# A small constant added to the softmax row sums by ACT instead of DVE, for the first twelve heads

## The chip, the core and the metric

The kernel runs on one core of a Trainium2 chip. The engines are named as in the profile: PE is TensorE (matrix products and transposes), DVE is VectorE, ACT is ScalarE, POOL is GpSimd, and SP is the queue from which nearly all transfers are issued. Each engine works through its own queue of instructions and waits on semaphores for what other engines or transfers deliver. The metric is the time of one execution on the device, in microseconds, as the median of several runs.

## The reference

Attention with a sliding window and a few always visible first keys ("sinks"), followed by a two-layer network:

```
scores = scale * q @ k.T                     # 4 batches, 8 heads, 768 positions, head size 64
keep = (key < n_sink) | (0 <= pos - key < window)      # n_sink 4, window 128
a = exp(where(keep, scores, -1e9) - max)
a = a / (sum(a) + 1e-09)
x = (a @ v) laid out as 3072 x 512
h = x @ w_in                                 # 512 x 2048
g = max(h, 0) + log1p(exp(-abs(h)))
out = g @ w_out                              # 2048 x 512, float32
```

The sum of `1e-09` and the row sum is the place of the change. The weights come in as 64-bit floats; all else is 32-bit.

## The kernel before

The 768 positions of each batch are cut into three chunks of 256 queries, twelve chunks in all, and each chunk is worked on as two blocks of 128 rows (j = 0, 1). A query block needs only its own 128 keys, the 128 before them, and the sinks, which fit into 136 columns since the two key blocks are folded into one by a mask (`copy_predicated`, line 270).

For one head h of a chunk the steps are named by letters:

- S, `scores`: PE multiplies queries and keys of both blocks into PSUM.
- T, `softmax` (lines 259 to 277): DVE folds and masks the scores and takes the row maximum into `stats` (lines 270, 276); ACT takes the exponential and sums each row into a column of `sm`, a 128 x 2 tile with one column for each block (line 277: an ACTIVATE and a read of the accumulator for each block).
- N, `normalise` (lines 279 to 291): DVE adds 1e-9 to `sm` (line 283) and takes the reciprocal into `rc` (line 284); then POOL, ACT or DVE multiplies the weights of both blocks by it (lines 289, 291), as a string of letters (`Ctx.NM`) says for each head; for heads 0 to 11 that is P P V A P A P P P A V P.
- W, `weights_t`: PE transposes the weights, ACT or DVE copies them out of PSUM into `th` (`Ctx.TH`), POOL selects the triangles into `pt`.
- k and K: the same for the sink columns. V, `values`: PE multiplies with the values. O, `out`: the result is split into a high part `xh` (ACT) and a low part `xl` (DVE or POOL).

The network part of a chunk has the steps U (first product), F (three ACT functions on a 128 x 512 tile), P and R (DVE's sum, the high part `gh` and the residue `gl`), D and E (second product). All products with 32-bit values run as sums of products of high and low parts.

The weights are turned into such parts only once, during the first chunks, in 32 halves (wi for the first layer, wo for the second): w issues the transfer on SP, a copies out the upper 16 bits (`upper`), c puts together a 32-bit word on DVE (line 434), d rounds it to the high part and l subtracts for the low part, on engines named by the strings `WT`, `WH` and `WL`.

The order is written out by hand. `Ctx.START` is a list of such letters with head numbers, for everything up to the point where a regular pattern (`Ctx.STEADY`) takes over, and every engine's queue keeps that order. Its beginning, which holds the twelve heads of the change (N0 to N11; heads 8 to 11 are the first four of the second chunk):

```
j4 w w w J0 S0 T0 G4 w S1 S2 w N0 L8 T1 T2 S3 w N1 L10 S4 W1 T3 a N2 W0 w T4 a N3 S5 k0 c c K0 a S6
w d c T5 d V0 V1 l N4 l W2 T6 w d O0 a G6 c S7 W3 O1 l N5 N6 T7 z18 V2 a a c N7 d W4 k4 S8 a T8 O2 w V3
c S9 c O3 w w K4 d a l l W5 V4 T9 S10 W6 L12 N9 V5 O4 d T10 w l N8 O5 W7 G8 d S11 w c T11 l a V6 V7
G10 a L14 N11 N10 O6 k8 w w c W8 O7 U0 d c l a d S12 ...
```

G and L are loads of values and of queries and keys, issued on SP in the same order as the weight transfers; z are products that fill PE's idle time. `sm` has two buffers, `rc` two.

Of the kernel before, what the change touches and what calls it, by code (L numbers as in the profile page):

```python
# [11 lines left out]
F32 = mybir.dt.float32  # L12
# [5 lines left out]
AF = mybir.ActivationFunctionType  # L18
ALU = mybir.AluOpType

B, H, S, D = 4, 8, 768, 64
DM, DFF = 512, 2048
P = 128
# [35 lines left out]
def _zero(nc, out, finite):  # L59
    nc.gpsimd.tensor_scalar(out, finite, 0.0, 0.0, ALU.mult, ALU.add)  # L60


def _turn(engines, k):

    return engines[min(k, len(engines) - 1)]
# [57 lines left out]
class _Attention:  # L123
# [155 lines left out]
    def normalise(self, h):  # L279
        c, nc = self.c, self.c.nc  # L280
        g, hh = h // G, h % G
        rc, sm = self.rc[g][:, :, hh], self.sm.pop(h)
        nc.vector.tensor_scalar(sm[:], sm[:], 1e-9, None, ALU.add)
        nc.vector.reciprocal(rc, sm[:])  # L284
        for j in range(CH):
            a = self.a[g][:, hh, j, :P]
            eng = _turn(c.NM, self.chunk * H + h)
            if eng == "A":
                nc.scalar.mul(a, a, rc[:, j : j + 1])
            else:  # L290
                (nc.vector if eng == "V" else nc.gpsimd).tensor_scalar(a, a, rc[:, j : j + 1], 0.0, ALU.mult, ALU.add)  # L291
# [544 lines left out]
def _general(c):  # L836

    tc, nc = c.tc, c.nc
    with ExitStack() as st:
        pool = lambda n, bufs: st.enter_context(tc.tile_pool(name=n, bufs=bufs))  # L840
        psum = lambda n, bufs: st.enter_context(tc.tile_pool(name=n, bufs=bufs, space=bass.MemoryType.PSUM))
        c.stg, c.gp, c.xp, c.mp = pool("gstg", 2), pool("gp", 1), pool("gxp", 1), pool("gmp", 1)
        c.ps_acc, c.ps_h, c.gs, c.gt, c.gx = psum("gacc", 1), psum("gh", 1), psum("gs", 1), psum("gt", 1), psum("gx", 1)
        _general_weights(c)
        keep = _general_masks(c)
        with tc.For_i(0, B, 1) as b:
            for n in range(NCH):
                xh, xl = c.x[n] = [c.xp.tile([P, 4, CT], F32R, tag=f"x{e}", name=f"gx{e}{n}") for e in "hl"]
                for h in range(H):
                    if h % 2 == 0:  # L850
                        xt = c.gx.tile([P, CT], F32, name=f"g_x{n}_{h}", tag="g_x")
                    _general_head(c, b, n, h, keep, xt)
                    if h % 2 == 1:
                        _copy(nc, "A", xh[:, h // 2], xt[:])
                        _sub(nc, "V", xl[:, h // 2], xt[:], xh[:, h // 2])
                m = _Moe(c, n)
                m.row = b * S + n * CT
                for s in range(FP):
                    m.up(s)
                    m.softplus(s)  # L860
                    m.gate(s)
                    m.residue(s)
                    for j in range(2):
                        m.down(s, j)


def _kernel(tc, a, out):
    nc = tc.nc
    c = Ctx()
    c.nc, c.tc, c.a, c.out = nc, tc, a, out  # L870
    c.E = dict(qkh="A", ql="V", kl="V", vh="A", vl="P", xh="A", xl="P", gl="V", out="AV")
    c.x, c.vs, c.vst, c.vsr, c.vsh = {}, {}, {}, {}, {}
    c.w64 = a["w"].dtype == mybir.dt.int64
    nc.scalar.preload_act_table_set("natural_log_exp_and_others")
    with ExitStack() as keep:
        c.const = keep.enter_context(tc.tile_pool(name="const", bufs=1))
        c.wp = keep.enter_context(tc.tile_pool(name="wp", bufs=1))
        c.w, c.raw, c.top, c.word = {}, {}, {}, {}
        c.ident = c.const.tile([P, P], F32, name="ident")
        c.stats = c.const.tile([P, B * H * NB], F32, name="stats")  # L880
        c.room = c.const.tile([P, 2, 4 * FP], F32, name="room")
        nc.gpsimd.memset(c.room[:], 1.0)
        c.sk = c.const.tile([P, CT], F32R, name="sk")
        ones = c.room[:].rearrange("p a b -> p (a b)").unsqueeze(1).broadcast_to([P, CT // 64, 64])
        _zero(nc, c.sk[:].rearrange("p (a b) -> p a b", b=64), ones)
        with ExitStack() as st:
            pool = lambda n, bufs: st.enter_context(tc.tile_pool(name=n, bufs=bufs))
            psum = lambda n, bufs: st.enter_context(tc.tile_pool(name=n, bufs=bufs, space=bass.MemoryType.PSUM))
            c.xp, c.mp, c.stg = pool("xp", 2), pool("mp", 2), pool("stg", 4)
            c.lp, c.ap, c.sp = pool("lp", 2), pool("ap", 2), pool("sp", 2)  # L890
            c.ps_acc, c.ps_h = psum("ps_acc", 1), psum("ps_h", 2)
            c.ps_s, c.ps_t, c.ps_x = psum("ps_s", 2), psum("ps_t", 1), psum("ps_x", 1)
            c.last = True
            with tc.manual_schedule(engines=ORDERED):
                _fast(c)
            c.last = False
        ok = nc.values_load(c.flag[:1, :1], min_val=0, max_val=1)
        with tc.If(ok < 1):
            _general(c)


Ctx.nchunks = B * NCH
Ctx.GB, Ctx.EXACT = 3, 2
Ctx.NM = "PPVAPAPPPAVPPAPVP"
Ctx.TH = "AAVVAAAAVAAAAAVVVA"
Ctx.GH = "AAVAVPPVV"
# [20 lines left out]
def build(nc, a, out):  # L927
    with tile.TileContext(nc, schedule_with_timeline_sim=True) as tc:
        _kernel(tc, a, out)
# [55 lines left out]
```

## Time and profile before

| what | value |
|---|---|
| median of 3 runs | 714.65 us (714.27 to 715.22) |
| the profiled execution's own time | 715.5 us |
| its span, first to last instruction | 713.7 us |
| PE busy | 691.6 us, 97% of the span |
| DVE busy | 574.2 us, 80% |
| ACT busy | 451.3 us, 63% |
| POOL busy | 373.7 us, 52% |
| granted TensorE clock | 0.997 of full speed |

Durations below are from the one profiled execution. A row of the timeline names the start in us from the span's start, the duration, the engine, the line of the kernel, the operation, what is written from what is read, and in brackets the idle time of the engine just before it with what ended that. Shares of busy time over the whole span mix the first part, in which weights are converted and the heads of the first chunks start, with the long regular part; the stretches are therefore read apart.

### The profile page before, as it was taken

Reading aid. Unit: us, or ns where it says so; the run is one execution under the profiler, and the core shown is the slowest. Engines: PE = TensorE matmul, PEld = TensorE weight load, DVE = VectorE, ACT = ScalarE, POOL = GpSimd, SP = SyncE. Lnnn points to the kernel's source line nnn. Section 1 sums busy time; section 2 is a strip of 40 time slices with the busy share of each in tenths; the row PEclk is TensorE's granted clock in tenths of the full one; section 3 lists DMA queues with packets and bytes.
Section 4 is the critical chain, followed back from the end, with each engine's and each line's share of the span. In section 5 each row is a group of like instructions: output and inputs, shape, how many; then the busy total and the mean of one; then the engine's idle time right before and its main releaser. Section 6 shows DMA issues by size and latency. Waiting matters only on the chain.

```text
span 713.7 us, 13800 instructions
## 1 busy us (share of the span) xinstructions
PE 691.6 (97%) x4519; PEld 624.8 (88%) x4519; DVE 574.2 (80%) x1663; ACT 451.3 (63%) x1105; POOL 373.7 (52%) x676
## 2 busy tenths in 40 slices
PE   6789899999999999999999999999999999999996
PEld 5678799989989999998999999998998989999995
DVE  5899988888888987888887887988888888865541
ACT  4679857667666666666666666766665765753431
POOL 5867586655555564654645554664554555452000
PEclk9999999999999999999999999999999999999998
DMA  8987613122221311411321321322222222100001
GB/s 308 326 329 237 209 51 98 52 73 77 63 76 56 97 50 50 124 52 46 102 68 49 109 63 56 93 65 65 76 76 66 83 62 67 61 12 1 30 1 35
DMA packets 39483, 64.52 MB, mean 90 GB/s; under 512 B 4650, under 2 KB 20074, under 8 KB 39402
## 3 DMA queue, kind: packets, MB, share of 16 engines
q1 hardware_dynamic: 38826, 63.02, 28.1%
q8 instruction: 38, 0.62, 0.4%
q10 hardware_dynamic: 576, 0.53, 0.2%
q14 instruction: 43, 0.35, 0.2%
HBM read 57.24 MB, written 6.29 MB: 89 GB/s over the span
## 4 chain that ended last, share of the span: by engine, by line
PE 89%; DMA 5%; ACT 2%; DVE 1%; POOL 1%; SPq 1%; issue 0%; POOLq 0%; DVEq 0%; ACTq 0%
PE h L490 37%; PE acc L541 12%; PE acc L542 12%; PE acc L543 12%; PE x L364 6%; PE s L255 3%; PE s L256 3%; PE t L324 2%; PE x L357 1%; DMA wi50r<-w 1%; DMA wo21r<-w 1%; DMA wi01r<-w 1%; DMA wo70r<-w 1%; DMA vz<-v 1%; PE ts L308 1%; ACT upper L48 0%
## 5 line engine op out<-in xcount | busy, mean ns | idle before, releaser
L490 PE MATMUL h<-xh,wi 128*128 128x256 f32 x1536 | 253.6, 288 | 0.0
L490 PEld LDWEIGHTS h<-xh,wi 128*128 128x128 f32 x1536 | 211.2, 191 | 0.9
L291 POOL TENSOR_SCALAR a<-a,rc 128x128 f32<-128x128 f32 x178 | 69.1, 401 | 188.8 <-DVE rc L284 156.1
L490 PE MATMUL h<-xl,wi 128*128 128x256 f32 x768 | 154.7, 283 | 0.0
L541 PE MATMUL acc<-wo,gh 128*128 128x512 f32 x384 | 151.9, 396 | 0.0
L543 PE MATMUL acc<-wo,gl 128*128 128x512 f32 x384 | 150.8, 393 | 0.7 <-DVE gl L56 0.7
L542 PE MATMUL acc<-wo,gh 128*128 128x512 f32 x384 | 150.8, 393 | 0.0
L490 PEld LDWEIGHTS h<-xl,wi 128*128 128x128 f32 x768 | 119.6, 192 | 0.0
L497 ACT ACTIVATE mt<-h 128x512 f32<-128x512 f32 x96 | 57.1, 595 | 97.5 <-PE h L490 97.4
L505 DVE SCALAR_TENSOR_TENSOR mt<-h,mt 128x512 f32<-128x512 f32 x96 | 66.1, 689 | 62.9 <-ACT mt L499 55.4
L277 ACT ACTIVATE a<-a,stats 128x136 f32<-128x136 f32 x192 | 76.2, 398 | 42.3 <-DVE stats L276 42.2
L543 PEld LDWEIGHTS acc<-wo,gl 128*128 128x128 f32 x384 | 72.2, 188 | 17.6 <-DVE gl L56 1.1
L541 PEld LDWEIGHTS acc<-wo,gh 128*128 128x128 f32 x384 | 72.2, 188 | 12.5
L542 PEld LDWEIGHTS acc<-wo,gh 128*128 128x128 f32 x384 | 72.4, 188 | 8.8
L56 DVE TENSOR_TENSOR gl<-mt,gh 128x512 fp32r<-128x512 f32 x96 | 79.4, 827 | 0.3
L335 POOL TENSOR_SCALAR_AFFINE_SELECT pt<-tl 128x256 fp32r<-128x256 f32 x80 | 60.0, 749 | 23.4 <-DVE tl L56 22.8
L498 ACT ACTIVATE mt<-mt 128x512 f32<-128x512 f32 x96 | 60.7, 633 | 3.1
L499 ACT ACTIVATE mt<-mt 128x512 f32<-128x512 f32 x96 | 60.7, 632 | 3.1
L335 POOL TENSOR_SCALAR_AFFINE_SELECT pt<-th 128x256 fp32r<-128x256 f32 (+1 forms) x96 | 43.7, 456 | 35.6 <-ACT th L48 32.7
L48 ACT CAST qkh<-qk 128x656 fp32r<-128x656 f32 x80 | 59.5, 744 | 2.0 <-DMA qk<-qk 2.0
L56 DVE TENSOR_TENSOR kl<-qk,qkh 128x400 fp32r<-128x400 f32 x80 | 51.6, 645 | 2.5
L56 DVE TENSOR_TENSOR tl<-t,th 128x256 f32<-128x256 f32 x80 | 33.2, 414 | 23.3 <-ACT th L48 23.3
(187 smaller groups left out, 1235.0 us busy)
## 6 DMA issues: line engine op xcount, KB each, us to landing
qk<-qk SPq DMA_DIRECT2D x160, 164.0 KB, 3.0
out<-o SPq DMA_DIRECT2D x23, 256.0 KB, 2.3
vr<-v SPq DMA_DIRECT2D x28, 192.0 KB, 2.6
q<-q SPq DMA_DIRECT2D x7, 256.0 KB, 5.5
k<-k SPq DMA_DIRECT2D x8, 200.0 KB, 4.8
vz<-v SPq DMA_DIRECT2D x4, 384.0 KB, 5.1
vr<-v SPq DMA_DIRECT2D x12, 128.0 KB, 2.3
vz<-v SPq DMA_DIRECT2D x4, 256.0 KB, 5.6
```

The lines of the kernel that those rows point to most:

```text
L48: nc.scalar.copy(out, in_)
L56: (nc.vector if eng == "V" else nc.gpsimd).tensor_tensor(out, a, b, ALU.subtract)
L277: nc.scalar.activation(a, a, AF.Exp, bias=nm, scale=-1.0, accum_out=sm[:, j : j + 1])
L291: (nc.vector if eng == "V" else nc.gpsimd).tensor_scalar(a, a, rc[:, j : j + 1], 0.0, ALU.mult, ALU.add)
L335: nc.gpsimd.affine_select(pt[:, e, :, 1], src[:], [[0, CH], [1, P]], ALU.is_ge, 0.0, base=0, channel_multiplier=-1)
L490: nc.tensor.matmul(h[:, j], wt, x, start=k == 0, stop=k >= len(prods) - 2, skip_group_check=True)
L498: nc.scalar.activation(t[:], t[:], AF.Exp, scale=-1.0)
L499: nc.scalar.activation(t[:], t[:], AF.Ln, bias=1.0)
L505: nc.vector.scalar_tensor_tensor(t[:], h[:], 0.0, t[:], ALU.max, ALU.add)
L541: nc.tensor.matmul(acc[:], gh[:, j, q], wh, start=f == 0, stop=False, skip_group_check=True)
L542: nc.tensor.matmul(acc[:], gh[:, j, q], wl, start=False, stop=False, skip_group_check=True)
L543: nc.tensor.matmul(acc[:], gl[:, j, q], wh, start=False, stop=f == 2 * FP - 1, skip_group_check=True)
```

## The change

For the first twelve heads, counted over chunks, ACT adds the constant: an Identity whose bias is a column filled once by POOL. All other heads keep DVE's add. The reciprocal stays on DVE.

```
         rc, sm = self.rc[g][:, :, hh], self.sm.pop(h)
-        nc.vector.tensor_scalar(sm[:], sm[:], 1e-9, None, ALU.add)
+        if self.chunk * H + h < c.SA:
+            nc.scalar.activation(sm[:], sm[:], AF.Identity, bias=c.eps[:, 0:1])
+        else:
+            nc.vector.tensor_scalar(sm[:], sm[:], 1e-9, None, ALU.add)
         nc.vector.reciprocal(rc, sm[:])
...
         nc.gpsimd.memset(c.room[:], 1.0)
+        c.eps = c.const.tile([P, 1], F32, name="eps")
+        nc.gpsimd.memset(c.eps[:], 1e-9)
...
-Ctx.GB, Ctx.EXACT = 3, 2
+Ctx.GB, Ctx.EXACT, Ctx.SA = 3, 2, 12
```

Neither `Ctx.START` nor any other order is edited; the Identity stands in ACT's queue where N_h stands in the list.

## The prediction

> **What bounds the kernel now.** I read the busy time of each engine in stretches first, then the chain of waits, then who waited for whom, and last the instructions of DVE and ACT in order of time up to 40 us.
>
> ```profile
> 39.00:87.00 48.00, 42.45 (x274) 37.29 (x274) 47.10 (x105) 41.88 (x89) 29.62 (x33) 1.00 0.74 254
> 87.00:640.00 553.00, 553.00 (x3681) 504.06 (x3681) 466.45 (x1359) 362.44 (x898) 311.32 (x573) 1.00 0.24 70
> ```
>
> The columns are the stretch, its length, then the busy time of PE, PE's weight loads, DVE, ACT and POOL, the granted clock, the DMA share and GB/s. From 87 to 640 us PE is busy for the whole 553.00 us: there nothing that DVE or ACT does is felt. From 39 to 87 us PE is not full (42.45 of 48.00), and DVE is (47.10). So the end is set by when PE's unbroken stretch begins, and that by DVE. The waits confirm both ends; first those of PE from 87 us to the end, then those of DVE from 38 to 95 us:
>
> ```profile
> PE x L364 <- POOL pt L338: 0.3, 1, 0.3
> ```
> ```profile
> DVE xl L56 <- ACT xh L48: 0.3, 1, 0.3
> ```
>
> PE's last wait of the whole run is 0.3 us long, at the start of the window. DVE waits 0.3 us in all between 38 and 95 us. Whatever DVE is late by at 39 us it therefore carries to 87 us, and PE with it to the end, unless something else was later still.
>
> **Where the changed instructions lie.** The add of line 283, for the window from 0 to 38.1 us:
>
> ```profile
> L283 DVE TENSOR_SCALAR sm<-sm x12: 149/170/608, 9.6 to 38.0; 128x2 f32<-128x2 f32 x12
> ```
>
> All twelve heads, N0 to N11 in the written order, are normalised before 38.1 us, ahead of the stretch in which DVE never rests. Nothing in the steady part is touched. What remains is what DVE and ACT do between 9 and 39 us; here are the rows that the sum uses, DVE's first. The columns are start, duration, engine, line, operation, operands and count.
>
> ```profile
> 9.63 0.17 DVE L283 TENSOR_SCALAR sm<-sm 128x2 f32<-128x2 f32 x1 [0.74 <-ACT a L277]
> 9.83 0.17 DVE L284 RECIPROCAL rc<-sm 128x2 f32<-128x2 f32 x1
> ...
> 11.56 0.17 DVE L284 RECIPROCAL rc<-sm 128x2 f32<-128x2 f32 x1
> ...
> 12.47 0.17 DVE L284 RECIPROCAL rc<-sm 128x2 f32<-128x2 f32 x1
> ...
> 13.49 0.08 DVE L276 DVE_READ_ACCUMULATOR2_ANT stats<- 128x1 f32 x1
> ...
> 14.68 0.52 DVE L50 CAST upper<-wi01r 128x512 f16<-128x512 bf16 x1 [0.89 <-DMA wi01r<-w]
> ...
> 15.51 0.17 DVE L284 RECIPROCAL rc<-sm 128x2 f32<-128x2 f32 x1
> ...
> 19.50 0.17 DVE L284 RECIPROCAL rc<-sm 128x2 f32<-128x2 f32 x1
> ...
> 23.81 0.28 DVE L283 TENSOR_SCALAR sm<-sm 128x2 f32<-128x2 f32 x1
> 24.12 0.17 DVE L284 RECIPROCAL rc<-sm 128x2 f32<-128x2 f32 x1
> ...
> 24.39 0.17 DVE L284 RECIPROCAL rc<-sm 128x2 f32<-128x2 f32 x1
> ...
> 32.52 0.17 DVE L284 RECIPROCAL rc<-sm 128x2 f32<-128x2 f32 x1
> ...
> 34.84 0.42 DVE L56 TENSOR_TENSOR xl<-x,xh 128x256 fp32r<-128x256 f32 x1 [0.71 <-ACT xh L48]
> ...
> 38.16 0.17 DVE L284 RECIPROCAL rc<-sm 128x2 f32<-128x2 f32 x1
> ```
> ```profile
> 11.92 0.18 ACT L277 ACTIVATION_READ_ACCUMULATOR a<-a,stats 128x1 f32 x1
> 13.03 0.37 ACT L48 COPY th<-t 128x256 f32<-128x256 f32 x1 [0.93 <-PE t L324]
> 13.30 0.41 ACT L277 ACTIVATE a<-a,stats 128x136 f32<-128x136 f32 x1
> ...
> 14.00 0.19 ACT L277 ACTIVATION_READ_ACCUMULATOR a<-a,stats 128x1 f32 x1
> ...
> 19.56 0.60 ACT L48 CAST wi<-wt 128x512 fp32r<-128x512 f32 x1
> ...
> 24.39 0.69 ACT L289 ACTIVATE a<-a,rc 128x128 f32<-128x128 f32 x2 [2.72 <-DVE sm L283]
> ...
> 32.78 0.37 ACT L48 COPY th<-t 128x256 f32<-128x256 f32 x1 [0.58 <-PE t L324]
> ...
> 34.46 0.35 ACT L48 CAST xh<-x 128x256 fp32r<-128x256 f32 x1
> ...
> 37.44 0.77 ACT L48 CAST upper<-wo11r 128x512 f16<-128x512 bf16 x1
> ...
> 47.47 0.62 ACT L48 CAST gh<-mt 128x512 fp32r<-128x512 f32 x1
> 48.00 0.79 ACT L48 CAST upper<-wo21r 128x512 f16<-128x512 bf16 x1
> ```
>
> The reader is to see that ACT's queue runs in the written order. Head 3's exponential begins at 13.30, behind the copy of W1 at 13.03, for which ACT sat idle 0.93 us waiting for PE, although DVE had moved on long before. An instruction put into ACT's queue at N_h is thus held by all that is written ahead of N_h: by the exponentials of a later head, and by copies that wait for PE.
>
> **The price of one Identity.** No Identity of this size is in the trace. From below, the smallest ACT row is the accumulator read (0.18 us at 11.92); from above, the multiply with a column operand, two of which fill 0.69 us at 24.39, on 128 columns instead of 2:
>
> ```profile
> L48 ACT CAST xh<-xf 128x256 fp32r<-128x256 f32 x40 | 16.3, 406 | 44.0 <-DVE xf L383 44.0
> L48 ACT CAST wi<-wt 128x512 fp32r<-128x512 f32 x11 | 6.7, 610 | 1.0 <-DVE wt L434 1.0
> L289 ACT ACTIVATE a<-a,rc 128x128 f32<-128x128 f32 x8 | 2.8, 394 | 3.2 <-DVE sm L283 2.7 <-DVE rc L284 0.4
> L874 ACT ACT_TABLE_LOAD x1 | 1.3, 1283 | 0.8 <-PEq L978 0.8
> ```
>
> One more column costs (610 - 406)/256 = 0.80 ns, so 126 fewer than the multiply's 394 ns leave 0.29 us. I take 0.29, with 0.19 and 0.39 as ends. After it the reciprocal starts 0.03 us later, as it did after the add (9.63 + 0.17 = 9.80, then 9.83): 0.32 us from the Identity's start. The next independent ACT instruction starts 0.10 us before its predecessor's end, as at 13.03 + 0.37 and 13.30.
>
> [...]
>
> **The change, head by head.** I push each step by the lateness so far, keep all other spacings, and write the lateness of the reciprocal against its old start.
>
> N0: the Identity takes the add's moment, 9.63; reciprocal at 9.95, late 0.12.
> N1 is written behind T1 and T2, so it stands behind the exponential of head 2, whose last read moves to 12.04. Identity 12.14, reciprocal 12.46 (was 11.56): late 0.90. POOL's normalisation of head 1, PE's transpose and ACT's copy of it (13.03) move with it, and so does head 3's exponential behind that copy, whose last read comes at 14.90.
> N2 is written behind T3, hence behind this exponential: Identity 15.00, reciprocal 15.32 (was 12.47): late 2.85. Before, the add of head 2 waited for nothing. Queued behind the waiting reciprocal on DVE are T4, the weight conversions and all later heads.
> N3 stands behind head 4's exponential. T4's first statistic is out at 13.57 + 2.85 = 16.42, the pair takes 0.70 to its last read (13.30 to 14.00): 17.15; Identity 17.25, reciprocal 17.57 (was 15.51): late 2.06. Part of the lateness is absorbed here, because the old DVE stood 0.89 us before 14.68 for a DMA.
> N4 stands behind the weight cast that ran at 19.56: that is 21.62 now, the Identity starts 22.12, reciprocal 22.44 (was 19.50): late 2.94.
> N5 finds its Identity done. DVE comes at 23.81 + 2.94 = 26.75 and goes on at once. N6 stands behind ACT's two multiplies of head 5, which wait for N5's reciprocal: they start 0.27 after it as before (24.12 to 24.39), at 27.02, and let go 0.59 later; Identity 27.61, reciprocal 27.93 (was 24.39): late 3.54.
> N7 finds its Identity done; the add's 0.20 (9.63 to 9.83) comes back: 3.34.
> N9 is written behind W6, whose copy ran at 32.78: 36.12, next instruction 36.39, reciprocal 36.71 (was 32.52): late 4.19.
> N8 is written behind T10 and takes the place of the cast at 34.46, now 38.65; the cast moves to 38.84, and the subtraction that waited for it (34.84) is late 4.38. The reciprocal, at 38.97, is not what DVE waits for last.
> N11 and N10 stand behind the conversion of 37.44: 41.82 plus 0.67, Identities at 42.49 and 42.68, reciprocal of N10 at 43.00 (was 38.16): late 4.84.
>
> DVE is thus 4.8 us late when its unresting stretch begins. The Identity's duration enters this some ten times (N0 to N4, N6, N9, N8 and both of the last pair), so its ends give 3.8 and 5.8. The constant column is one more memset of POOL at the start. I cost it at nothing: nobody reads it before the first Identity at 9.63, where DVE sits waiting anyway (0.74 us in its row); without that cover it would cost its own length, which no row shows for one column and which I bound by the 0.17 us of DVE's add. SP issues no new DMA, but its loads of later heads wait for PE's scores of earlier ones and move with DVE by 2 to 4 us.
>
> The profiled execution took 715.5 us around a span of 713.7; with 4.8 more it is a span of 718.5 and a time of 720.3. The three runs have their median 0.85 below the profiled one, at 714.65, so the forecast there is **719.4 us**.
>
> **Rivals.** A: DVE is relieved and the kernel is faster. Each add held DVE 0.20 us, twelve of them 2.4, and the slowest (608 ns) some 0.4 more: 712.0. [...] For it speaks that DVE is full and ACT is not. It holds where ACT has passed N_h before DVE comes, and in the rows that is so for N5 and N7 alone. It would decide if ACT's queue did not hold the Identities back. Chance 0.09.
>
> B: The weight DMAs decide from 39 us on, so only their delay counts. The chain of waits says this:
>
> ```profile
> 31.37 7.99 DMA wo21r<-w
> 39.36 0.02 issue
> 39.38 8.64 DMA wi50r<-w
> 48.02 0.77 ACT upper L48
> ```
>
> The delay would be that of the loads issued behind T5, 2.06 us: 716.7. Against it, the instruction at 48.00 converts wo21r, landed at 39.36, and ACT was busy right up to it (47.47 + 0.62 - 0.10 = 47.99); nothing waited there. Chance 0.10.
>
> C: No change, because something I hold to be in step with DVE had slack and swallows the 4.8 us. DVE's waits above show 0.3 us of it. 714.6, chance 0.07.
>
> D: Identity is not in the loaded table set, and each one brings two table loads of 1.28 us: about ten on the path, 26 us, 740. The multiplies of line 289 ran with one load in the whole trace. Chance 0.02.
>
> **How the numbers follow.** The forecast has the remaining 0.72. The range takes in its ends (718.4 and 720.4) with some 0.8 more above for shifted collisions on DVE, whose adds vary from 149 to 608 ns, and rival B below with 0.5 for the same reason: 716.2 to 721.2. Outside lie A, C and D, 0.18. A measurement of this kernel can tell 0.2%, 1.4 us, from no change. Slower than that are the forecast, B and D: 0.84; same 0.07; faster 0.09.
>
> **What would show it.** Right: DVE's reciprocals wait for ACT some 10 us in all before 45 us, where the adds waited for two exponentials before; the longest single wait, over 2 us, stands at N2 behind head 3's exponential; the reciprocal of N10 starts near 43.0; from there all rows are the old ones shifted by one amount, and PE's last wait lies near 91.5 us. Wrong: the Identities start out of the written order, or the shift at N10 is 4.8 us and that at PE's last wait much smaller, or the reciprocals come earlier than before.

## The result, and the profile after

The changed kernel takes 721.63 us (median of six runs, 720.17 to 723.55) against 714.46 us before (six runs beside them): +7.2 us, a ratio of 1.0104 [1.0093, 1.0115]. It is slower. The forecast was 719.4 with a range up to 721.2; the time lies 0.4 above that range. The profiled execution took 722.55 us around a span of 720.7 and a mean granted clock of 0.993 (before: 715.5, 713.7, 0.997).

First the busy time in stretches, in the same columns as before:

```profile
9.00:39.00 30.00, 20.67 (x101) 16.36 (x100) 19.11 (x78) 17.31 (x64) 16.96 (x34) 0.89 0.84 305
39.00:87.00 48.00, 40.68 (x254) 34.99 (x253) 45.51 (x114) 41.43 (x97) 30.56 (x37) 1.00 0.77 265
87.00:100.00 13.00, 12.73 (x87) 11.62 (x87) 12.73 (x30) 11.34 (x24) 9.34 (x11) 1.00 0.32 90
100.00:640.00 540.00, 540.00 (x3595) 491.81 (x3594) 456.18 (x1334) 354.21 (x878) 305.05 (x561) 1.00 0.24 71
```

The steady part is as it was: PE is busy for the whole of 100 to 640 us. The loss lies in the first row. Its clock column reads 0.89, which the prediction had not reckoned with. The same row of the kernel before:

```profile
9.00:39.00 30.00, 23.26 (x130) 18.15 (x130) 25.94 (x112) 20.68 (x75) 22.53 (x42) 1.00 0.96 356
```

There DVE did 25.94 us of work in these 30 us, now 19.11; the clock was whole. DVE's waits between 8 and 46 us of the changed kernel, then PE's from 87 us to the end:

```profile
DVE rc L287 <- ACT sm L284: 12.6, 9, 3.7
DVE wt L437 <- ACT upper L48: 0.3, 1, 0.3
DVE th L50 <- POOL pt L341: 0.2, 1, 0.2
```
```profile
PE x L367 <- POOL pt L341: 0.3, 1, 0.3
```

DVE's reciprocal (line 287 now) waits nine times for ACT's Identity (line 284), 12.6 us in all. The Identity itself is as cheap as assumed, and there is still one table load in the whole trace (1.28 us, as before):

```profile
L284 ACT ACTIVATE sm<-sm,eps 128x2 f32<-128x2 f32 x12 | 3.4, 289 | 0.1
```

The lateness at 39 us goes to the end undiminished. In the changed kernel, the reciprocals of N11 and N10, and PE's last wait of the run:

```profile
44.97 0.35 DVE L287 RECIPROCAL rc<-sm 128x2 f32<-128x2 f32 x2 [0.64 <-ACT sm L284]
...
93.76 1.14 PE L367 MATMUL x<-pt,vz 128*128 128x128 f32 x6 [0.27 <-POOL pt L341]
```

and PE's last wait in the kernel before:

```profile
86.78 1.14 PE L364 MATMUL x<-pt,vz 128*128 128x128 f32 x6 [0.26 <-POOL pt L338]
```

The second of the pair, N10, starts at about 45.15 (44.97 + 0.18), 7.0 after the old 38.16; PE's last wait comes 6.98 later; the span is 7.0 longer. So DVE's lateness is carried to the end as forecast, and it is about 2 us larger.

### The profile page after: what moved, and what is told of

The parts are those of the page before. It is cut to its first block, busy times and chain, and to the rows that moved or that the text cites. A ratio compares the mean times of both kernels' runs of the same rounds, so it can differ in the third digit from the quotient of the medians.

```text
span 720.7 us, 13798 instructions
## 1 busy us (share of the span) xinstructions
PE 694.9 (96%) x4519; PEld 626.9 (87%) x4519; DVE 572.6 (79%) x1651; ACT 454.5 (63%) x1117; POOL 374.8 (52%) x677
## 4 chain that ended last, share of the span: by engine, by line
PE 87%; DVE 5%; ACT 4%; issue 1%; POOL 1%; DMA 1%; ACTq 0%; POOLq 0%; DVEq 0%
PE h L493 36%; PE acc L544 12%; PE acc L545 12%; PE acc L546 12%; PE x L367 5%; PE t L327 3%; PE s L255 3%; PE s L256 3%; PE x L360 1%; ACT a L277 1%; ACT upper L48 1%; DVE wt L437 1%; PE ts L311 1%; DMA words<-sizes 1%; ACT wi L48 0%
## 5 line engine op out<-in xcount | busy, mean ns | idle before, releaser
L544 PEld LDWEIGHTS acc<-wo,gh 128*128 128x128 f32 x384 | 72.1, 188 | 12.6
L56 DVE TENSOR_TENSOR gl<-mt,gh 128x512 fp32r<-128x512 f32 x96 | 77.8, 811 | 0.2
L338 POOL TENSOR_SCALAR_AFFINE_SELECT pt<-th 128x256 fp32r<-128x256 f32 (+1 forms) x96 | 45.2, 471 | 36.9 <-ACT th L48 33.9
```

Of the source, the lines that this page charges most:

```text
L56: (nc.vector if eng == "V" else nc.gpsimd).tensor_tensor(out, a, b, ALU.subtract)
L338: nc.gpsimd.affine_select(pt[:, e, :, 1], src[:], [[0, CH], [1, P]], ALU.is_ge, 0.0, base=0, channel_multiplier=-1)
L544: nc.tensor.matmul(acc[:], gh[:, j, q], wh, start=f == 0, stop=False, skip_group_check=True)
```

## The experiments

Three theories were to be told apart. **Queue:** an Identity at N_h in ACT's queue is held by what is written ahead of it, DVE waits, and the wait is carried 1:1. **Load:** the twelve instructions are too much for ACT wherever they stand, or the step is slow as such. **Clock:** DVE's waits leave PE idle, its granted clock falls, and slower PE steps lengthen the waits; this would be the part that the forecast lacks.

### The same Identity at another place, and the same load without the wait

`e1_early12` issues the Identity at the end of T, right behind the accumulator reads of its own head:

```
 # softmax, behind the loop over j
+if chunk * H + h < c.SA:
+    nc.scalar.activation(sm[:], sm[:], AF.Identity, bias=c.eps[:, 0:1])
 # normalise
+if self.chunk * H + h >= c.SA:
     nc.vector.tensor_scalar(sm[:], sm[:], 1e-9, None, ALU.add)
```

> The same twelve Identities on ACT, but each written right behind its own head's exponentials instead of at the head's normalise step. If the place in ACT's queue made the change slow, nothing is left in front of an Identity but its own head: DVE gets back 0.2 us and more at most heads and the time is 711.5 to 713.5 us, 1 to 3 us under the kernel before. If it is the longer latency of an add on ACT, or ACT's extra work, it stays slow: 717 us or more.

`e2_dummy` keeps DVE's add and issues an Identity at N_h that reads a constant and writes a scratch tile that nobody reads:

```
 nc.vector.tensor_scalar(sm[:], sm[:], 1e-9, None, ALU.add)
+if self.chunk * H + h < c.SA:
+    nc.scalar.activation(c.junk[:], c.room[:, 0, :2], AF.Identity, bias=c.eps[:, 0:1])
```

> The kernel before with DVE's add kept, and twelve Identities of the same size on ACT at the same places that read a constant and write a scratch tile nobody reads. If DVE's waiting is the cause, ACT's own load is worth little: 714.3 to 715.3 us. If ACT's extra instructions are the cause, most of the 7 us is there: 718 to 722 us.

Measured: `e1_early12` 715.79 us, ratio 1.0013 [1.0002, 1.0023]; `e2_dummy` 715.12 us, ratio 1.0005 [0.9994, 1.0016]. Twelve more instructions on ACT cost nothing that can be measured, and the add done by ACT costs 0.1 to 1.6 us when it isn't held by later work, where the change costs 7.2. Load falls, Queue stands. But `e1_early12` was also expected to gain from the adds that DVE no longer does, and did not. DVE's waits in it, between 8 and 46 us:

```profile
DVE rc L287 <- ACT sm L279: 3.0, 4, 1.1
DVE th L50 <- POOL pt L341: 1.8, 1, 1.8
DVE xl L56 <- ACT xh L48: 1.3, 1, 1.3
DVE wt L437 <- ACT upper L48: 0.3, 1, 0.3
DVE upper L50 <- DMA wi01r<-w: 0.2, 1, 0.2
```

The kernel before had waits of 3.4 us in this window; here they are 6.6. What DVE no longer computes it waits for: ACT, and POOL behind it, don't come earlier because DVE does. One place shows in the rows, the word that DVE puts together for `wi10r`:

```profile
17.23 1.26 POOL L56 TENSOR_TENSOR wi<-wt,wi 128x512 fp32r<-128x512 f32 x1 [1.37 <-DVE wi L50]
...
17.34 1.71 DVE L437 SCALAR_TENSOR_TENSOR wt<-wi10r,upper 128x512 int32<-128x512 int32 x1 [0.25 <-ACT upper L48]
```

DVE has to wait 0.25 us for ACT's cast of `wi10r`, starts 0.11 behind a subtraction of POOL and takes 1.71 us. In the kernel before it starts at 17.62, 0.01 ahead of POOL, and takes 0.69. With both executions lined up on the last accumulator read of head 0 (9.41 in the kernel before, 9.06 here), N3's reciprocal is 0.16 us early, N4's 0.45 late, and PE's last wait (87.15) 0.72 late. The loss thus arises between N3 and N4, at this word, while the granted clock is 1.00. The later waits weren't taken apart one by one.

`e2_dummy` starts its first reciprocal at 9.36, the changed kernel at 9.37 (the kernel before at 9.83, since its transfer of `sizes` landed later). It is the ruler for lateness below. The ruler is not quite the kernel before: lined up on head 0's last accumulator read (8.85 against 9.41), its N10 is 0.45 us late and its PE's last wait 0.42, since the dummy Identities of N9 and N8 stand ahead of ACT's cast to `xh`, and DVE's subtraction behind that waits 1.09 instead of 0.71.

### The waiting of PE filled with idle products

`e3_after_fill` is the changed kernel with more of the products z, which fill PE's idle time and whose results nobody reads, at the places where PE now waits:

```
-... N3 S5 k0 c c K0 a S6
+... N3 S5 k0 c c z20 K0 a S6
-... N5 N6 T7 z18 V2 ...
-c S9 c O3 w w K4 d a l l W5 V4 ...
+... N5 N6 T7 z26 V2 ...
+z9 c S9 c O3 w w K4 d a l l z4 W5 V4 ...
```

> The changed kernel with idle-time products added on PE where it stood waiting: 20 ahead of K0, 8 more ahead of V2, 9 ahead of S9, 4 ahead of W5. They write a PSUM tile that is overwritten later. If the part of the slowdown above the forecast comes from PE's granted clock falling after its waits (0.50 at 18 to 20 us, 0.52 at 34 to 36 us), the clock stays near 1.00 there and the time falls to 718.9 to 720.2 us. If the low clock is only a bystander, it stays at 721 to 722 us, or gets worse by the work added.

`e4_before_nofill` is the counter-test: the kernel before without its own z18, so that its clock falls where nothing else is changed.

```
-... N5 N6 T7 z18 V2 ...
+... N5 N6 T7 V2 ...
```

> The kernel before without the 18 idle-time products ahead of V2, so that PE stands idle for some 3.5 us between 20.4 and 24 us, with no Identity anywhere. If a wait of PE costs a low clock afterwards and that reaches the end, the clock shows below 0.8 somewhere between 22 and 32 us and the time rises by 0.5 to 2 us, to 715.0 to 716.5 us. If the low clock does not matter, the time stays at 714.3 to 714.8 us.

`e9_fill_first` has only the z20 ahead of K0, `e10_fill_second` only the z26, z9 and z4.

> The changed kernel with the first of the four groups of idle-time products alone, 20 ahead of K0. If the two falls of PE's clock cost separately, the first through the sink transpose, ACT's conversion behind it and the collision of DVE's word with POOL's subtraction, this takes back some 1.2 us of the changed kernel's loss: 6.0 us over the kernel before, 720.0 to 721.0 where that shows 714.5, the word of wi10 at 0.69 us; a second fall near 33 to 37 us may remain. If the first fall is a bystander, it stays 7 us over.

> The changed kernel with the other three groups alone (8 more ahead of V2, 9 ahead of S9, 4 ahead of W5). If the second fall costs through W6's late transpose, in front of N9's Identity, this takes back some 1.4 us: 5.6 to 6.2 us over the kernel before, the wait at N9 near 2.0 us in place of 3.7; the clock still falls near 18 to 20 us and the word of wi10 still takes 1.6 us. If only the first fall counts, it stays 7 us over.

Measured: `e3_after_fill` 719.95 us (1.0071 [1.0057, 1.0085]), `e9_fill_first` 719.91 (1.0067 [1.0054, 1.0081]), `e10_fill_second` 720.08 (1.0071 [1.0057, 1.0085]), `e4_before_nofill` 715.38 (1.0005 [0.9995, 1.0016]). The stretches in which the clock fell; the changed kernel, then with all the fillers:

```profile
16.00:18.00 2.00, 0.25 (x2) 0.22 (x3) 1.34 (x6) 1.70 (x7) 0.00 (x0) 0.75 1.02 405
18.00:20.00 2.00, 2.00 (x8) 1.70 (x7) 1.65 (x4) 1.10 (x3) 0.70 (x1) 0.50 0.88 352
...
34.00:36.00 2.00, 2.00 (x7) 1.64 (x7) 1.21 (x7) 2.00 (x7) 1.59 (x2) 0.52 0.93 321
36.00:38.00 2.00, 2.00 (x9) 1.68 (x8) 0.00 (x0) 0.01 (x1) 0.29 (x2) 0.63 1.08 389
```
```profile
16.00:18.00 2.00, 1.45 (x13) 1.27 (x12) 1.36 (x8) 1.52 (x7) 0.16 (x1) 1.00 1.03 416
18.00:20.00 2.00, 2.00 (x12) 1.64 (x12) 1.85 (x4) 1.29 (x3) 0.53 (x1) 1.00 0.93 370
...
34.00:36.00 2.00, 2.00 (x12) 1.66 (x11) 0.22 (x3) 1.41 (x8) 1.31 (x3) 1.00 1.04 408
36.00:38.00 2.00, 1.09 (x8) 0.78 (x7) 1.35 (x8) 1.43 (x7) 1.93 (x3) 1.00 1.03 402
```

In the first fence PE is busy for 0.25 of the 2 us to 18.00 and then has a clock of 0.50; in the second it is kept busy and the clock stays whole. PE's last wait, of `e2_dummy` and of `e3_after_fill`:

```profile
86.64 1.14 PE L366 MATMUL x<-pt,vz 128*128 128x128 f32 x6 [0.27 <-POOL pt L340]
```
```profile
91.09 1.14 PE L367 MATMUL x<-pt,vz 128*128 128x128 f32 x6 [0.27 <-POOL pt L341]
```

The execution of `e3_after_fill` begins 0.20 us later (first reciprocal at 9.56), so with the clock whole up to 38 us the lateness is 91.09 - 86.64 - 0.20 = 4.25 us, where the changed kernel has 7.1. (One fall is left in `e3_after_fill`, behind 38 us: the clock is 0.88 from 38 to 40 us and 0.96 over 39 to 87 us. N10 is no later there than in `e12_changed_again` below, whose clock is 1.00 in both stretches.) In the profile of `e9_fill_first` only the second fall is left (0.50 from 34 to 36 us) and the lateness is 5.9 (PE's last wait at 93.07, begun 0.55 later); in that of `e10_fill_second` only the first (0.50 from 18 to 20 us), and it is 5.3 (91.93). Taken from 7.1, this puts the first fall at 1.2 us and the second at 1.8; taken against the 4.25, at 1.0 and 1.6. The word of `wi10r` takes 0.69 us in `e9_fill_first` and 1.61 in `e10_fill_second`, and N9 waits 3.68 and 2.01 us, as was expected of each. The medians of the three filled kernels don't separate: where a fall lands differs between executions, as the last experiment shows. The profiled execution of `e9_fill_first` took 722.04 us, its four others 718.71 to 720.20.

The cost of a fall of the clock differed with who waits for PE. In `e4_before_nofill`, at a place where DVE does not:

```profile
24.00:26.00 2.00, 2.00 (x10) 1.79 (x9) 1.97 (x10) 1.95 (x8) 2.00 (x2) 0.70 1.02 371
26.00:28.00 2.00, 2.00 (x6) 1.51 (x5) 1.93 (x11) 1.29 (x4) 1.79 (x5) 0.50 0.99 377
```

DVE stays full there (1.97 and 1.93 of 2.00). N9's add then waits 1.12 us for ACT instead of 0.82; with the first reciprocals lined up (9.51 and 9.83), PE's last wait is 0.28 late (86.74). So this fall costs 0.3 us, which the time, with its interval from -0.4 to 1.1 us, can't show. A loss of 0.5 to 2 us had been expected if the low clock reaches the end; that was too much.

How long PE has to stand idle before its clock falls is not shown by any run here. Read in finer slices, the changed kernel's clock is 1.00 from 8 to 17.00 us and 0.50 from 17.10 to 20.40, then 1.00 from 20.60 to 34.00 and 0.50 from 34.10 to 37.40: 3.3 us each time. The first fall comes within PE's wait of 2.92 us ahead of K0, the second while PE is busy, behind waits of 1.26 and 0.51 us (up to 32.01 and 33.86). In `e3_after_fill` PE waits 0.55 us ahead of K0 and the clock stays at 1.00. The moment of a fall differed between two executions of one program (see the last experiment).

### Which heads it is

Only the set of heads is changed; for the others DVE's add stays:

```
-if self.chunk * H + h < c.SA:
+if self.chunk * H + h in (0, 5, 7):        # e5_heads057
+if self.chunk * H + h in (8, 9, 10, 11):   # e6_heads8to11
+if self.chunk * H + h < 8:                 # e7_heads0to7
```

> The changed kernel with ACT's Identity for heads 0, 5 and 7 alone, DVE's add for the rest. These are the heads at which, by the working, ACT is past the place before DVE comes (5 and 7) or the place is the add's own (0). If the wait behind other work in ACT's queue is the cause, they cost nothing: 714.2 to 715.4 us. If each Identity costs alike (7.2 us over twelve, 0.6 each), it is 1.8 us: 716.3 to 717.2 us.

> Identity for heads 8 to 11 alone. The working gives, from a DVE that is on time, 0.85 us at N9 (behind W6's copy), 1.04 in the subtraction behind N8, 1.5 at N10: 716.0 to 717.2 us with the clock whole, and no clock fall ahead of 30 us. If each Identity costs alike: 2.4 us, 717 to 718.

> Identity for heads 0 to 7 alone. The working gives 3.3 us with the clock whole (718.2); with PE's clock falling after its wait ahead of K0, as in the changed kernel, and the collision on DVE that followed, 1.2 more: 718.0 to 720.0 us. If the falls of the clock belong to the first eight heads and not to the last four, the fall near 34 to 37 us is here too.

Measured: 715.55 us (1.0013 [1.0001, 1.0026]), 717.17 (1.0031 [1.0018, 1.0043]) and 719.41 (1.0065 [1.0052, 1.0078]); over their own runs of the kernel before that is +0.8, +2.4 and +4.7 us. The three heads for which the forecast saw hardly any wait (0, 5, 7) cost 0.8 us between them; three equal shares of 7.2 would be 1.8. The two groups that make up the whole change add to 7.1. By the times alone equal shares are not excluded: the interval of the first reaches up to 1.9 us, and 2.4 and 4.7 are what four and eight shares would be (2.4 and 4.8). The profiles decide. In `e5_heads057` no reciprocal but N0's waits for an Identity (1.13 us, where N0's add waited 0.74 in the kernel before), and lined up on head 0's last accumulator read (8.77 and 9.41), PE's last wait (86.02) is 0.1 us earlier than in the kernel before. In `e7_heads0to7` the reciprocals of heads 0 to 4 and 6 wait, 7.3 us in all, those of 5 and 7 not at all; the clock falls near 18 to 20 us (0.50) and is 1.00 from 34 to 38. The price of a head is set by its place; what the 0.8 us of the first median come from isn't shown.

### What the removed adds were worth

`e8_both` has the Identity at N_h and keeps DVE's add behind it; the constant is added twice.

```
+if self.chunk * H + h < c.SA:
+    nc.scalar.activation(sm[:], sm[:], AF.Identity, bias=c.eps[:, 0:1])
 nc.vector.tensor_scalar(sm[:], sm[:], 1e-9, None, ALU.add)
```

> The twelve Identities on ACT where the change puts them, and DVE's add kept as well behind each (the constant is added twice for these heads). Only the wait is added here and no work taken from DVE. If the waiting is everything, the time is the changed kernel's or up to 2 us above it, since the adds that fall away do so mostly within waits: 721 to 724 us. If the change's own gain, the removed adds, hides a larger loss, it is more than 2 us above.

Measured: 725.31 us, 1.0149 [1.0134, 1.0163], +10.6 us. That is 3.4 us more than the change, where twelve adds behind a wait, on the path with their full length, would be 2.4 by the forecast's 12 x 0.20. So an add behind a wait does hold DVE. How much of the 3.4 is the adds stays open: in the profile of `e8_both` the clock also fell more (0.83 over 9 to 39 us against the 0.89 of the changed kernel, with 0.50 from 18 to 24 us), and executions of the changed kernel differ by as much (below).

`e11_early1to7` was to keep this relief and avoid the wait: the Identity at the end of T as in `e1_early12`, for heads 1 to 7 alone.

```
 # softmax, behind the loop over j
+if 0 < chunk * H + h < 8:
+    nc.scalar.activation(sm[:], sm[:], AF.Identity, bias=c.eps[:, 0:1])
 # normalise
+if not 0 < self.chunk * H + h < 8:
     nc.vector.tensor_scalar(sm[:], sm[:], 1e-9, None, ALU.add)
```

> ACT's Identity right behind the head's own exponentials, for heads 1 to 7 alone; DVE's add for all others. With twelve heads this came out level with the kernel before, with DVE then waiting for ACT at N9 and in the subtraction behind N8. If those two waits ate the gain, leaving heads 8 to 11 alone keeps it: 1 to 2 us faster than before, 712.5 to 713.5. If DVE's time saved at heads 1 to 7 is lost again ahead of N9, to POOL's triangles and the collisions, it is level: 714.0 to 715.0.

Measured: 716.38 us, 1.0023 [1.0012, 1.0033]. No gain; the time is above both expected ranges, though the second named the place, ahead of N9. DVE's waits at N9 and behind N8 are as in the kernel before, 0.8 and 0.7 us, but the word of `wi10r` again starts 0.11 us behind POOL's subtraction and takes 1.71 us. Lined up as for `e1_early12` (last accumulator read of head 0 at 8.78), N3's reciprocal is 0.23 early, N4's 0.39 late and PE's last wait (86.94) 0.79 late. So the gain of these two versions is lost mainly at one collision of DVE with POOL. A version that avoids it wasn't run, and none that beats the kernel before was found.

### The changed kernel once more

`e12_changed_again` is the changed kernel with nothing altered.

> The changed kernel as it is, profiled a second time and timed in more rounds, since its runs lie 3.4 us apart where those of the kernel before lie 1.4. If the falls of PE's clock come from its waits alone, they stand at the same places again: 0.50 near 18 to 20 us and 34 to 37 us, a wait of 3.7 us at N9, a span 6 to 8 us longer. If where a fall lands is partly chance, one of the two is missing or elsewhere, the wait at N9 is near 2.0 without the second, and the runs again spread over 2 us or more, their lowest near the forecast 719.4.

Measured: 720.52 us over six executions from 718.75 to 723.13, 1.009 [1.0073, 1.0107]; the profiled one took 718.75, 3.8 less than that of the first profile. The same program, so the two traces show what differs by chance. The stretch around K0, first in the 722.55 us execution, then in the 718.75 us one:

```profile
17.75 0.59 PE L311 MATMUL ts<-ident,sa 128*32 128x128 f32 x2 [2.92 <-DVE sa L299]
...
18.43 0.36 ACT L48 COPY sk<-ts 32x256 f32<-32x256 f32 x1 [0.35 <-PE ts L311]
18.70 0.76 ACT L48 CAST upper<-wi10r 128x512 f16<-128x512 bf16 x1
...
19.30 1.26 POOL L56 TENSOR_TENSOR wi<-wt,wi 128x512 fp32r<-128x512 f32 x1 [3.31 <-DVE wi L50]
...
19.49 1.62 DVE L437 SCALAR_TENSOR_TENSOR wt<-wi10r,upper 128x512 int32<-128x512 int32 x1 [0.35 <-ACT upper L48]
```
```profile
17.80 0.38 PE L311 MATMUL ts<-ident,sa 128*32 128x128 f32 x2 [2.91 <-DVE sa L299]
...
18.27 0.36 ACT L48 COPY sk<-ts 32x256 f32<-32x256 f32 x1
18.54 0.76 ACT L48 CAST upper<-wi10r 128x512 f16<-128x512 bf16 x1
...
19.33 0.69 DVE L437 SCALAR_TENSOR_TENSOR wt<-wi10r,upper 128x512 int32<-128x512 int32 x1
19.34 1.81 POOL L56 TENSOR_TENSOR wi<-wt,wi 128x512 fp32r<-128x512 f32 x1 [3.31 <-DVE wi L50]
```

In both, PE waits 2.9 us before K0. In the first the clock has already fallen (0.75 from 16 to 18 us) and the transpose takes 0.59; in the second it falls a moment later (1.00 to 18 us, then 0.54) and the transpose takes 0.38. With 0.59, ACT's copy waits 0.35, the cast of `wi10r` starts 0.16 later, and DVE's word comes 0.19 behind POOL's subtraction instead of 0.01 ahead of it. In these two, whichever starts first keeps its time and the other is stretched: POOL 1.26 and DVE 1.62, or DVE 0.69 and POOL 1.81. DVE is the one that is waited for, and N4's reciprocal starts at 23.25 in the first, at 22.16 in the second: 1.1 us out of 0.2. The same holds in all fourteen profiles: in the six in which POOL starts first, by 0.11 to 0.20 us, the word takes 1.61 to 1.71, in the eight others 0.69. Why the one stretches the other, the rows don't show.

The second difference is at N9, again the 722.55 us execution and then the other:

```profile
36.32 1.64 PE L252 MATMUL s<-k,q 128*128 128x264 f32 x4
...
38.29 0.37 ACT L48 COPY th<-t 128x256 f32<-128x256 f32 x1 [2.28 <-PE t L327]
38.56 0.30 ACT L284 ACTIVATE sm<-sm,eps 128x2 f32<-128x2 f32 x1
...
38.89 0.17 DVE L287 RECIPROCAL rc<-sm 128x2 f32<-128x2 f32 x1 [3.69 <-ACT sm L284]
```
```profile
34.11 1.06 PE L252 MATMUL s<-k,q 128*128 128x264 f32 x4
...
35.50 0.37 ACT L48 COPY th<-t 128x256 f32<-128x256 f32 x1 [0.59 <-PE t L327]
35.77 0.30 ACT L284 ACTIVATE sm<-sm,eps 128x2 f32<-128x2 f32 x1
...
36.10 0.17 DVE L287 RECIPROCAL rc<-sm 128x2 f32<-128x2 f32 x1 [2.01 <-ACT sm L284]
```

N9 stands behind W6, whose copy waits for PE's transpose, which PE does after the scores S10. Where the clock has fallen (0.52 and 0.63 from 34 to 38 us) S10 takes 1.64 instead of 1.06 and PE's two steps ahead of it 1.07 and 1.49 instead of 0.60 and 0.82; the copy waits 2.28 instead of 0.59, and the reciprocal 3.69 instead of 2.01: 1.7 us. In the second execution this fall did not happen (1.00 from 34 to 38 us). 1.1 and 1.7 are the difference at PE's last wait, 93.76 - 90.89 = 2.9. Some 1.0 of the 3.8 us lies behind PE's last wait and is no part of the change: from there to the end of the span it is 626.9 us in the first execution and 625.9 in the second, 626.9 in the kernel before and 626.0 in `e2_dummy`. The issue of the last transfer, on ACT's queue, takes 1.66 us in the first and 1.67 in the kernel before. Why the clock fell at one moment in one execution and not in the other is not settled.

## Why the prediction was right, and where it was wrong

Lateness in us, each reciprocal (and PE's last wait) against `e2_dummy`, with the executions lined up on the first reciprocal, so that N0's own lateness of 0.1 us is not in the measured columns:

| step | forecast | first profile of the change | `e12_changed_again` | `e3_after_fill` |
|---|---|---|---|---|
| N1 | 0.90 | 0.77 | 0.75 | 0.76 |
| N2 | 2.85 | 2.65 | 2.62 | 2.63 |
| N3 | 2.06 | 2.13 | 2.09 | 2.12 |
| N4 | 2.94 | 4.20 | 3.03 | 3.06 |
| N6 | 3.54 | 4.67 | 3.48 | 3.52 |
| N7 | 3.34 | 4.29 | 3.10 | 3.13 |
| N9 | 4.19 | 6.92 | 4.05 | 4.07 |
| N10 | 4.84 | 7.1 | 4.2 | 4.2 |
| PE's last wait | | 7.11 | 4.16 | 4.25 |

**What bounds the kernel** was right: lateness at 39 us reaches the end 1:1 in every column.

**The place in the queue** was right: with the same Identity elsewhere, or held but not waited for, the loss is gone or nearly so (`e1_early12`, `e2_dummy`). The Identity's 0.29 us was measured at 0.289. The memset of the constant column, costed at nothing, took 0.10 us on POOL at 0.9 us, and nothing waited for it.

**The head-by-head sum** was right where no fall of the clock lengthened a wait: to within 0.25 us through N9 in the last two columns. The 0.6 at N10 is in the main the ruler's, which is itself late there. Against the kernel before, lined up on head 0's last accumulator read (9.41, and 8.83 in `e12_changed_again`), N10 is 42.34 - 38.16 + 0.58 = 4.76 us late where 4.84 was forecast, PE's last wait 90.89 - 86.78 + 0.58 = 4.69, and no step in between is off by more than 0.3.

**The step that failed** is "keep all other spacings". It took each instruction's duration and each engine's order as fixed. In fact DVE's waits left PE idle, its clock fell to 0.50, and PE steps that the new waits hang on became longer (the sink transpose 0.59 instead of 0.38 us, S10 1.64 instead of 1.06): 1.2 us at N4 by way of the collision on DVE and POOL, 1.7 more by N9 (the steps in the table's third column over the fourth and fifth). The range had 0.8 us above the sum's end "for shifted collisions", on DVE alone; there was nothing in it for the clock. Whether a given execution has one such fall, both, or a harmless one differed between the two that were profiled, and the twelve executions of the changed kernel reach from 718.75 to 723.55 us. That the first median lies above the range and the second, 720.52, within it is chance; the term was missing either way.

**What would show it:** the waits of the reciprocals came to 10.9 us and 12.6 us where some 10 were named. The one at N2 was 2.00 and 1.99 us, just short of what was expected, and N9's was longer (3.69 and 2.01). N10 was to start near 43.0: 45.15 and 42.3. PE's last wait was to lie near 91.5: 93.76 and 90.89. One execution lies on either side of the forecast; both start some 0.6 us earlier than the kernel before did, which the forecast could not know.

**The rivals.** A, relief, was wrong as the outcome. An add does hold DVE (`e8_both`), but no version turned its removal into a gain. (By its own terms, 2.4 and 608 - 170 ns from 714.65, its time is 711.8 and not 712.0.) B, the weight transfers decide: wrong, as PE's last wait moved by the whole lateness, not by part of it. C, slack that swallows it: wrong for the same reason. D, table loads: wrong, there is one.

## What to carry to other kernels

An instruction moved to a less busy engine is priced by its place in that engine's queue: list what is written ahead of it, what each of these waits for, and who waits for the moved result; here a 0.29 us instruction cost up to 2 us of waiting (3.7 with PE's clock low), and next to nothing once its result was not waited for. A forecast that shifts a timetable by hand should then ask which other engine is left idle by the new waits, and price the steps behind that idle time at the lower clock too (0.50 here), wherever somebody waits for them. And a program whose executions differ by 3 us deserves a second profile before its loss is explained by one.

## What the runs showed of the hardware

The granted clock of PE fell to 0.50 twice in the first profile of the change, for 3.3 us each time: from 17.10 us, within a wait of 2.92 us, and from 34.10 us, behind waits of 1.26 and 0.51 us. It cost 1 to 2 us where the result of the slowed steps was waited for on the path to DVE, 0.3 in `e4_before_nofill`, and nothing from 18 to 22 us in `e12_changed_again`. DVE's word of 128 x 512 took 0.69 or 1.6 to 1.7 us and POOL's subtraction of the same size 1.81 or 1.26, decided by which of them started first by 0.2 us or less; so 0.2 us of delay on a third engine became 1.1.
